# Pooled attention with an expert layer: order of the first loads and layouts, and the last block's additions

## The chip, the cores and the metric

The program runs on one core of one Trainium2 chip. The metric is the device time of one execution in microseconds (us); smaller is better. Work is done by TensorE (PE; its weight loads are shown as PEld), VectorE (DVE), ScalarE (ACT) and GpSimd (POOL). SyncE (SP) issues most of the DMA transfers, ACT issues a few at the start.

## The reference

Queries are averaged in pairs along the sequence, attention with a softmax over 1152 keys follows, and the result of the eight heads of each batch entry goes through an expert layer with a squared rectifier.

```python
def _attn_ref(q, k, v):                      # 4 x 8 x 1152 x 64 each
    q_pool = q.reshape(B, H, S // factor, factor, D).mean(axis=3)
    scores = scale * np.matmul(q_pool, k.transpose(0, 1, 3, 2))
    scores = scores - np.max(scores, axis=-1, keepdims=True)
    attn = np.exp(scores)
    attn = attn / (np.sum(attn, axis=-1, keepdims=True) + 1e-09)
    return np.matmul(attn, v).astype(np.float32)
...
def _moe_ref(x, w_in, w_out, s, b):          # x: 2304 x 512, d_ff 2048
    h = x @ w_in
    r = np.maximum(h, 0.0)
    g = s * (r * r) + b
    return (g @ w_out).astype(np.float32)
```

## The kernel before

**Precision.** Most products are made of three passes on rounded parts: a number is split into a high part (rounded by ACT or POOL, `hi_of`, L285 and L287) and a low part (the difference, on DVE or POOL).

**Attention.** The 32 heads are worked on as 16 pairs. For each pair, `load_k` (L525) and `load_q` (L533) bring raw keys (four transfers) and queries (eight), in packets of 128 bytes. `prep_pair` adds the two queries of a pair of rows (`qs`), transposes keys (`ka`, `kb`, one half each) and queries (`qt`) on DVE, rounds them (`ha`, `hb`, `qh` on ACT; `qm` and `qz` are copies of the queries laid out for the maxima), and takes the low parts on POOL (`kl`, `ql`). `lay` (L579 to L582) then copies high and low parts with transfers into `kk` (keys) and `qq` (queries) of one head: these are the operands of the scores.

**Maxima.** Before a head's scores can be exponentiated, each query needs a bound. `max_unit` (L633, L634) multiplies one tile of queries with 384 keys and reduces the result to a maximum on DVE; a pair has 27 such units (9 tiles of queries by 3 blocks of keys), the first 15 belong to the pair's first head. When a head's units are done, `shift` reduces them to `c` (L652) and two small transfers (L657, L658) write `c` into a row of that head's `qq`. **The scores of a head therefore wait for the transfers of its `c`.** `begun(n)` is the number of units done before step n; 22 of pair 0's units are done ahead of step 0, and 27 before step 3.

**The main loop** has a step for each head and block of 128 keys (9 steps a head). In it stand four score products (`score_step`, L672, into `s`), the products with the values for the block three steps earlier (`value_step`, L704 to L714, into `o`), and some units of the next pair's maxima. Everything on an engine, and everything that SP issues, runs in the order in which the code recorded it: an instruction that waits holds up all that are behind it on that engine. Preparations of later pairs are put into steps by tables: `LD = 4` means that in step 4 the raw keys and queries of pair 2 are issued (`load_k(2)`, `load_q(2)`). Work given to `later(k, fn)` is recorded k ticks later, and a step ends with a tick. A transfer also waits for an earlier one when it takes over that one's completion semaphore (eight are used in turn).

**Start.** Keys, queries and values of pair 0 are loaded in this order, six of the eight transfers of queries by ACT. POOL clears buffers meanwhile. Then come all preparations of pair 0, the loads of pair 1, the layouts of heads 0 and 1, and the units ahead. Head 0's `c` is sent by ACT, all later ones by SP.

**Expert layer and tail.** The last stage works on pairs of expert blocks: `pair1` (L404 to L435) makes the rounded operands, `pair2` (L452) seven products into the four accumulators `a`, `b`, `m`, `z` (tiles `seven`), and after the last pair of a token block `drain` (L465) adds them on DVE into `yq`, nine additions, and two transfers (L482) write the block out. In the last token block nothing else is left to run beside this.

Of the kernel before, what the change touches and what calls it, by code (L numbers as in the profile page):

```python
# [52 lines left out]
LAGS = 2  # L53
# [7 lines left out]
def attention_moe_kernel(ctx: ExitStack, tc: tile.TileContext, q, k, v, w_in, w_out, s_in, b_in, out):  # L61
# [243 lines left out]
    class Moe:  # L305
# [89 lines left out]
        def pair1(self, blk, n):  # L395
# [43 lines left out]
        def pair2(self, blk, n, first, last):  # L439
# [5 lines left out]
            todo = ((a, 0, sums[0], w[1]), (a, 512, own[0], w[2]), (b, 0, own[1], w[3]), (b, 512, sums[1], w[4]), (m, 0, sums[4], w[0]), (m, HD, sums[3], w[5]), (z, 0, sums[2], w[6]))  # L445
            for at, (y, to, (gh, gl), (wh, wl)) in enumerate(todo):
# [6 lines left out]
                if last:  # L453
                    self.drain(blk, at)
# [3 lines left out]
        def drain(self, blk, at):  # L458
# [5 lines left out]
            def add(out, b, op=ALU.add):  # L464
                nc.vector.tensor_tensor(out=out, in0=out, in1=b, op=op)  # L465

            if at == 1:
                add(quad[:, 0::3], both(a))
                add(quad[:, 1], a[:, 512:512 + HD])
                add(quad[:, 1], a[:, :HD], ALU.subtract)  # L470
            elif at == 3:
                add(quad[:, 0::3], both(b))
                add(quad[:, 2], b[:, :HD])
                add(quad[:, 2], b[:, 512:512 + HD], ALU.subtract)
# [47 lines left out]
    def load_k(p):  # L522
        kraw[p] = ap.tile([P, NB, 32], F32, tag="kraw", name=f"kraw{p}")
        for r, b, h, c in quarters(p):
            nc.sync.dma_start(kraw[p][r], k[b, h, :, c].rearrange("(j t) i -> t j i", t=32))  # L525
# [14 lines left out]
    def prep_pair(p):  # L540
# [17 lines left out]
        def k_hi(part, last):  # L558
            hi_of(nc.scalar if p < 3 else nc.gpsimd, kh[:, part], kT[:, part])
            if last:  # L560
                khs[p] = kh
# [5 lines left out]
        def q_blocks():  # L567

            for h in range(2):
                r = slice(h * D, (h + 1) * D)  # L570
                hi_of(nc.scalar if p == 0 else nc.gpsimd, qzs[p % 2][r, h].rearrange("p (t m) -> p t m", t=NT4), qT[r, :NT4 * P].rearrange("p (m t) -> p t m", t=NT4))

        def lay(h):
# [3 lines left out]
            ks = ((f32(kk[D:P, 0, :]), kT[r]), (f32(kk[0:D]), f32(kh[r]).unsqueeze(1).to_broadcast([D, 2, S])))  # L577
            for dst, src in ks[::-1] if hd == 0 else ks:
                nc.sync.dma_start(dst, src)  # L579
            nc.sync.dma_start(f32(qq[0:D, 0, :]), f32(qh[r]))  # L580
            nc.sync.dma_start(f32(qq[D:P, 0, :]), f32(qh[r]))
            nc.sync.dma_start(f32(qq[0:D, 1, :]), qT[r])  # L582
# [10 lines left out]
            "qz": q_blocks,  # L593
            "kl": lambda: nc.gpsimd.tensor_tensor(out=kT, in0=kT, in1=f32(kh), op=ALU.subtract),
# [22 lines left out]
    def max_unit(u, pool, tag):  # L617
# [4 lines left out]
        t, e = divmod(w, NE)  # L622
# [16 lines left out]
    def begun(n):  # L639

        u = (n + AHEAD) * NU // 18
        if n > 0:
# [3 lines left out]
    def shift(hd, pm, full, rest):  # L646
# [7 lines left out]
        eng = nc.scalar if hd == 0 else nc.sync  # L654
# [104 lines left out]

    load_k(0)  # L760
    load_q(0)
    load_v(0)

# [21 lines left out]
    zeros(1)  # L785
    constants(1)
# [7 lines left out]
    prep_v(0)  # L794
    ones(1)
    constants(2)
    for n in range(AHEAD):
        for u in range(begun(n - AHEAD), begun(n - AHEAD + 1)):
            max_unit(u, *((ps_m, "m") if u % 2 == 0 else (ps_s, "s")))
        tick()  # L800
        if n == 11:
# [180 lines left out]
```

## Time and profile before

| | us |
|---|---|
| runs (three) | 917.39, 917.93, 918.42; median 917.93 |
| the profiled execution | 918.26, of which the span is 916.3 |
| PE, DVE, POOL, ACT busy in the span | 893.6 (98%), 690.8 (75%), 631.2 (69%), 570.3 (62%) |
| granted TensorE clock, mean | 0.995 |
| first product on PE, last product on PE (start) | 12.19, 910.16 |

The profile lists what each engine did, when, and what released an engine that had waited. "Granted clock" is the share of full speed at which TensorE ran: 1.00 is 2.4 GHz, 0.50 is 1.2 GHz. A DMA's row shows how long the issuing queue was occupied, not the transfer; "to landing" is from issue to arrival.

### The profile page before, as it was taken

The numbers are of one execution on the slowest core, as the hardware profiler recorded it, in microseconds if no ns is written. First come the engines' busy times: TensorE is split into PE (matmuls) and PEld (weight loads), VectorE is DVE, ScalarE is ACT, GpSimd is POOL, SyncE is SP. The second block draws the span as 40 slices with busy tenths as digits, with TensorE's granted clock in tenths as the row PEclk, the third lists the DMA queues.
The fourth block names the chain that finished last, engine by engine and source line by source line (L and its number), as shares of the span: only waits on it lengthen the run. The fifth ranks groups of instructions, "written<-read, shape, count | busy, mean of one in ns | idle before, by whom it ended". The sixth has DMA issues, their size and how long they took to land.

```text
span 916.3 us, 17038 instructions
## 1 busy us (share of the span) xinstructions
PE 893.6 (98%) x6036; PEld 830.5 (91%) x6036; DVE 690.8 (75%) x1271; ACT 570.3 (62%) x1050; POOL 631.2 (69%) x535
## 2 busy tenths in 40 slices
PE   4999999999999999999999999999999999999996
PEld 2889999999999999999998899989999999999996
DVE  5787888888888888888875678789884456666665
ACT  2766666767676767667668677766664445444442
POOL 8577766887788778877857667569985445554542
PEclk9999999999999999999999999999999999999999
DMA  8899788878877897888572465757643222222111
GB/s 151 158 170 197 156 171 168 158 167 165 175 149 172 162 180 145 174 161 168 125 176 73 151 207 177 250 179 223 185 139 121 87 69 71 70 70 69 48 47 47
DMA packets 255796, 131.22 MB, mean 143 GB/s; under 512 B 203872, under 2 KB 227424, under 8 KB 255712
## 3 DMA queue, kind: packets, MB, share of 16 engines
q1 hardware_dynamic: 251936, 129.69, 60.2%
q8 instruction: 48, 0.79, 0.4%
q10 hardware_dynamic: 3776, 0.45, 0.3%
q14 instruction: 36, 0.29, 0.1%
HBM read 68.68 MB, written 18.87 MB: 96 GB/s over the span
## 4 chain that ended last, share of the span: by engine, by line
PE 86%; DVE 7%; ACT 2%; POOL 1%; issue 1%; DMA 0%; SPq 0%; POOLq 0%; ACTq 0%; DVEq 0%
PE s L672 14%; PE y L379 11%; PE h L352 11%; PE h L404 11%; PE seven L452 9%; PE o L704 8%; PE m L633 8%; PE o L712 5%; PE o L714 5%; PE o L710 5%; DVE pm L634 2%; DVE yq L465 1%; DVE lt L732 1%; DVE rr L742 1%; DVE pl L687 1%
## 5 line engine op out<-in xcount | busy, mean ns | idle before, releaser
L634 DVE TENSOR_REDUCE pm<-m 128x1 f32<-128x384 f32 x432 | 226.2, 544 | 55.5 <-PE m L633 49.6
L672 PE MATMUL s<-qq,kk 128*128 128x288 f32 x1152 | 214.9, 309 | 1.2 <-ACT pe L676 0.4
L672 PEld LDWEIGHTS s<-qq,kk 128*128 128x128 f32 x1152 | 175.5, 189 | 11.8 <-DVE pl L687 1.3
L681 ACT ACTIVATE ph<-s 128x576 fp32r<-128x576 f32 x192 | 125.2, 652 | 96.3 <-PE s L672 95.7
L687 POOL TENSOR_TENSOR pl<-pe,ph 128x576 fp32r<-128x576 f32 x64 | 90.7, 1417 | 97.6 <-ACT pe L684 75.2
L633 PE MATMUL m<-kh,qz 128*128 128x384 f32 x384 | 154.5, 416 | 1.1 <-DVE pm L634 0.3
L704 PE MATMUL o<-pe,vf 128*128 128x288 f32 x384 | 120.6, 405 | 0.0
L687 DVE TENSOR_TENSOR pl<-s,ph 128x576 fp32r<-128x576 f32 x128 | 96.1, 751 | 31.6 <-ACT s L684 23.3
L712 PE MATMUL o<-ph,vl 128*64 128x288 f32 (+1 forms) x384 | 113.5, 295 | 0.2 <-POOL vl L608 0.2
L714 PE MATMUL o<-pl,vv 128*128 128x288 f32 x384 | 113.4, 295 | 0.1
L710 PE MATMUL o<-ph,vv 128*128 128x288 f32 x384 | 113.2, 295 | 0.0
L352 PE MATMUL h<-x,wih 128*128 128x256 f32 x576 | 106.8, 283 | 0.8 <-DVE gl L366 0.7
L404 PE MATMUL h<-x,wih 128*128 128x256 f32 x576 | 104.2, 281 | 0.0
L352 PEld LDWEIGHTS h<-x,wih 128*128 128x128 f32 x576 | 93.7, 190 | 7.7 <-DVE gl L366 1.9
L432 POOL TENSOR_TENSOR cl<-c,ch 128x640 fp32r<-128x640 f32 x36 | 56.4, 1567 | 57.5 <-ACT ch L428 57.5
L633 PEld LDWEIGHTS m<-kh,qz 128*128 128x128 f32 x384 | 72.7, 192 | 18.3 <-DVE pm L634 10.2
L404 PEld LDWEIGHTS h<-x,wih 128*128 128x128 f32 x576 | 88.7, 188 | 0.2
L676 ACT ACTIVATE pe<-s 128x576 f32<-128x576 f32 x96 | 62.6, 652 | 36.1 <-PE s L672 32.3
L684 ACT ACTIVATE s<-s 128x576 f32<-128x576 f32 x128 | 83.3, 651 | 0.0
L352 PE MATMUL h<-x,wil 128*128 128x256 f32 x288 | 81.6, 283 | 0.0
L330 POOL TENSOR_TENSOR x<-xr,x 128x1024 fp32r<-128x1024 f32 x27 | 65.0, 2406 | 23.7 <-ACT x L285 23.7
L404 PE MATMUL h<-x,wil 128*128 128x256 f32 x288 | 81.1, 282 | 0.0
(282 smaller groups left out, 2184.6 us busy)
## 6 DMA issues: line engine op xcount, KB each, us to landing
kk<-kh SPq DMA_DIRECT2D x32, 576.0 KB, 5.7
kraw<-in_k_dram SPq DMA_DIRECT2D x64, 144.0 KB, 3.4
vf<-in_v_dram SPq DMA_DIRECT2D x32, 288.0 KB, 4.2
kk<-kT SPq DMA_DIRECT2D x32, 288.0 KB, 3.5
qq<-qh SPq DMA_DIRECT2D x64, 144.0 KB, 5.6
xr<-xd SPq DMA_DIRECT2D x18, 512.0 KB, 3.9
qraw<-in_q_dram SPq DMA_DIRECT2D x122, 72.0 KB, 2.6
wsti<-in_moe_w_in_dram SPq DMA_DIRECT2D x13, 512.0 KB, 4.2
```

What stands on the lines that cost most here:

```text
L352: nc.tensor.matmul(h[:, :TB], st[:, c, :], mv[:, c, :], start=(n == 0), stop=(n == 3 * NC - 1))
L379: nc.tensor.matmul(y[:, :DM], st[:, ts_], mv, start=(first and n == 0), stop=(last and n == 2))
L404: nc.tensor.matmul(h[:, e * TB:(e + 1) * TB], st[:, c, :], mv[:, c, :], start=(k == 0), stop=(k == 3 * NC - 1))
L633: nc.tensor.matmul(ps[:, :KB], st, khs[p][:, e * KB:(e + 1) * KB], start=True, stop=True)
L634: nc.vector.tensor_reduce(out=pms[p][:, col, e:e + 1], in_=ps[:, :KB], axis=AX.X, op=ALU.max)
L672: nc.tensor.matmul(ps[:, a, :HALF], kk[:, i, j * P:(j + 1) * P], qq[:, i, a], start=(i == 0), stop=(i == 1))
L681: nc.scalar.activation(ph, ps[:, :, :HALF], AF.Exp, scale=SCALE)
L687: fresh.append(lambda: eng.tensor_tensor(out=pl, in0=full, in1=f32(ph), op=ALU.subtract))
L704: nc.tensor.matmul(o[:, :HALF], vfs[hd % 2][:, j], ph[:, a], start=first, stop=last)
L710: nc.tensor.matmul(o[:, :HALF], vv[:, j], ph[:, a], start=first, stop=False)
L712: nc.tensor.matmul(o[0:vl.shape[2], :HALF], vl[:, j], ph[:, a], start=False, stop=False)
L714: nc.tensor.matmul(o[:, :HALF], vv[:, j], pl[:, a], start=False, stop=last)
```

## The change

Four things are edited.

- **Start.** `load_q(0)` comes ahead of `load_k(0)`, alternating between SP and ACT; the keys come in two halves. The preparation is ordered queries first, then the first half of the keys. After the second unit of maxima the second half is prepared and head 0's layout is issued in pieces, then the loads of pair 1's keys. One of the two `qz` copies moves to POOL, the buffers of heads 1 and 2 are cleared later, and `load_q(1)` and head 1's layout follow `c` of head 0.
- **Maxima of head 0** go by key blocks: all five query tiles with keys 0 to 383, then the next block. Head 0's `c` is now sent by SP.
- **Units ahead.** `begun` gives 20 units ahead of step 0 instead of 22; 21, 23, 24, 26 and 27 are done before steps 1 to 5, so pair 0's last unit is in step 4, where it was in step 2.
- **Tail.** In every block `pair2` takes the two products with `ah`, `al` first. In the last pair of the last block `cl` is made on DVE; three of the nine additions go to POOL, from copies that ACT makes of the accumulators, and each half of the rows is written out when it is done.

```diff
-            todo = ((a, 0, sums[0], w[1]), (a, 512, own[0], w[2]), (b, 0, own[1], w[3]), (b, 512, sums[1], w[4]), (m, 0, sums[4], w[0]), (m, HD, sums[3], w[5]), (z, 0, sums[2], w[6]))
+            todo = ((a, 512, own[0], w[2]), (b, 0, own[1], w[3]), (a, 0, sums[0], w[1]), (b, 512, sums[1], w[4]), (m, 0, sums[4], w[0]), (m, HD, sums[3], w[5]), (z, 0, sums[2], w[6]))
...
-                nc.gpsimd.tensor_tensor(out=cl, in0=c, in1=f32(ch), op=ALU.subtract)
+                (nc.vector if end else nc.gpsimd).tensor_tensor(out=cl, in0=c, in1=f32(ch), op=ALU.subtract)
...
+            def single(k, bank, tag):
+                plus, minus, eng = bank[:, (k == 1) * 512:(k == 1) * 512 + HD], bank[:, (k == 2) * 512:(k == 2) * 512 + HD], nc.vector
+                if end and k == 2:
+                    add(quad[:, k], minus, ALU.subtract)
+                if end:
+                    t = self.q.tile([P, 5 * P if tag == "c" else 2 * TB], F32, tag=tag, bufs=1, name=f"end{k}")
+                    if k == 1:
+                        nc.scalar.activation(t[:, :2 * HD].rearrange("p (e d) -> p e d", d=HD), both(bank), AF.Copy)
+                        minus = t[:, :HD]
+                    else:
+                        nc.scalar.activation(t[:, :HD], plus, AF.Copy)
+                    plus, eng = t[:, (k == 1) * HD:(k == 1) * HD + HD], nc.gpsimd
+                add(quad[:, k], plus, ALU.add, eng)
+                if not end or k == 1:
+                    add(quad[:, k], minus, ALU.subtract, eng)
-            if at == 1:
+            if at == 2:
                 add(quad[:, 0::3], both(a))
-                add(quad[:, 1], a[:, 512:512 + HD])
-                add(quad[:, 1], a[:, :HD], ALU.subtract)
+                single(1, a, "c")
...
-                for i in range(TB // P):
-                    row = blk * TB + i * P
-                    later(1, lambda i=i, row=row: nc.sync.dma_start(out[row:row + P, :], acc[:, i]))
+            if at > 4:
+                i = at - 5
+                later(1, lambda: nc.sync.dma_start(out[blk * TB + i * P:blk * TB + (i + 1) * P, :], acc[:, i]))
...
-                eng = nc.sync if p or (r.start == P - 32) else nc.scalar
+                eng = nc.sync if p or e == 0 else nc.scalar
...
-        t, e = divmod(w, NE)
+        t, e = divmod(w, NE) if u >= (NT4 + 1) * NE else divmod(w, NT4 + 1)[::-1]
...
         u = (n + AHEAD) * NU // 18
+        if n < 7:
+            u = min(u, 20 + max(0, n * 3 // 2))
...
-        eng = nc.scalar if hd == 0 else nc.sync
+        eng = nc.sync
...
-    load_k(0)
     load_q(0)
+    load_k(0, 2)
     load_v(0)
...
-    for name in ("ka", "ha", "kb", "hb", "qs", "qt", "qm", "qz", "qh", "kl", "ql"):
+    for name in ("qs", "qt", "qm", "qz0", "ka", "ha", "qh", "kla"):
         prep[name]()
-    load_k(1)
-    prep["l0"]()
-    load_q(1)
-    prep["l1"]()
...
             max_unit(u, *((ps_m, "m") if u % 2 == 0 else (ps_s, "s")))
+            if u == 1:
+                for name in ("kb", "hb", "ql", "klb", "l0"):
+                    prep[name]()
+                load_k(1)
...
         tick()
+        if n == 10:
+            assert holds["c", 0] == 0
+            load_q(1)
+            prep["l1"]()
```

Three places in the order of instructions. **DVE at the start of the program**, before; `kraw0`, `qraw0` are the raw loads of pair 0, `m0_0` is the first unit of maxima:

```order
L586 STREAM_TRANSPOSE kT0_139<-kraw0_109 128x576
L588 STREAM_TRANSPOSE kT0_139<-kraw0_109 128x576
L587 TENSOR_TENSOR qs0_141<-qraw0_114 128x576
L590 STREAM_TRANSPOSE qT0_140<-qs0_141 128x576
L634 TENSOR_REDUCE pm0_190<-m0_0_191 128x1
```

The same place, DVE after:

```order
L625 TENSOR_TENSOR qs0_140<-qraw0_109 128x576
L628 STREAM_TRANSPOSE qT0_139<-qs0_140 128x576
L624 STREAM_TRANSPOSE kT0_138<-kraw0_118 128x576
L676 TENSOR_REDUCE pm0_152<-m0_0_153 128x1
L676 TENSOR_REDUCE pm0_152<-m0_1_156 128x1
L626 STREAM_TRANSPOSE kT0_138<-kraw0_118 128x576
```

The transpose of the second half of the keys moved behind the first two reductions, the queries moved to the front.

**SP between the layout of head 1 and that of head 2**, before; `kk1`, `qq1` are head 1's operands, `c1` its maxima, `kraw2` and `qraw2` the loads of pair 2:

```order
L582 DMA qq1_98<-qT0_140 64x576
L538 DMA vf1_104<-in_v_dram 128x9x64
L804 DMA sb_71<-in_moe_s_dram 128x1
L805 DMA sb_71<-in_moe_b_dram 128x1
L657 DMA qq1_98<-c1_315 1x128x4
L658 DMA qq1_98<-c1_315 1x64x1
L525 DMA kraw2_355<-in_k_dram 32x36x32 x4
L533 DMA qraw2_360<-in_q_dram 32x18x32 x8
```

The same place, SP after:

```order
L620 DMA qq1_98<-qT0_139 64x576
L555 DMA vf1_104<-in_v_dram 128x9x64
L853 DMA sb_71<-in_moe_s_dram 128x1
L854 DMA sb_71<-in_moe_b_dram 128x1
L543 DMA kraw2_360<-in_k_dram 32x36x32 x4
L550 DMA qraw2_365<-in_q_dram 32x18x32 x8
L701 DMA qq1_98<-c1_352 1x128x4
L702 DMA qq1_98<-c1_352 1x64x1
```

The two transfers of `c1` moved from ahead of the twelve loads of pair 2 to behind them.

**DVE's last instructions of the program**, before; `yq8_27` is the last block's sum, `seven0` to `seven3` are the accumulators `a`, `b`, `m`, `z`:

```order
L431 TENSOR_TENSOR gl8_14s_11935<-rr8_3_11930,gh8_14s_11934 128x256
L465 TENSOR_TENSOR yq8_27_11703<-yq8_27_11703,seven0_9699 128x2x256
L465 TENSOR_TENSOR yq8_27_11703<-yq8_27_11703,seven0_9699 128x256 x2
L465 TENSOR_TENSOR yq8_27_11703<-yq8_27_11703,seven1_9700 128x2x256
L465 TENSOR_TENSOR yq8_27_11703<-yq8_27_11703,seven1_9700 128x256 x2
L465 TENSOR_TENSOR yq8_27_11703<-yq8_27_11703,seven2_9701 128x2x256
L465 TENSOR_TENSOR yq8_27_11703<-yq8_27_11703,seven2_9701 128x256
L465 TENSOR_TENSOR yq8_27_11703<-yq8_27_11703,seven3_9702 128x256
```

The same place, DVE after (`cl8_3` is the last block's `cl`):

```order
L431 TENSOR_TENSOR gl8_14s_11942<-rr8_3_11937,gh8_14s_11941 128x256
L432 TENSOR_TENSOR cl8_3_11940<-c8_3_11938,ch8_3_11939 128x640
L465 TENSOR_TENSOR yq8_27_11710<-yq8_27_11710,seven0_9706 128x2x256
L465 TENSOR_TENSOR yq8_27_11710<-yq8_27_11710,seven1_9707 128x2x256
L465 TENSOR_TENSOR yq8_27_11710<-yq8_27_11710,seven1_9707 128x256
L465 TENSOR_TENSOR yq8_27_11710<-yq8_27_11710,seven2_9708 128x2x256
L465 TENSOR_TENSOR yq8_27_11710<-yq8_27_11710,seven2_9708 128x256
L465 TENSOR_TENSOR yq8_27_11710<-yq8_27_11710,seven3_9709 128x256
```

`cl8_3` moved from POOL to DVE, and three of DVE's nine additions moved to POOL.

## Rows read from the trace of the kernel before

**Rows 1.** The page's chain that ended last, shares of the span.

```profile
PE 86%; DVE 7%; ACT 2%; POOL 1%; issue 1%; DMA 0%; SPq 0%; POOLq 0%; ACTq 0%; DVEq 0%
```

**Rows 2.** Timeline of the start: start, us, engine, line, operation, [idle before].

```profile
8.53 0.78 DVE L586 STREAM_TRANSPOSE kT<-kraw 128x576 f32<-128x576 f32 x1 [8.53 <-DMA kraw<-in_k_dram]
...
9.34 1.34 ACT L285 ACTIVATE kh<-kT 128x576 fp32r<-128x576 f32 x2 [3.59 <-DVE kT L586]
...
12.19 1.30 PE L633 MATMUL m<-kh,qm 128*128 128x384 f32 x3 [12.19 <-ACT qm L285]
...
12.88 7.06 DVE L634 TENSOR_REDUCE pm<-m 128x1 f32<-128x384 f32 x15 [1.46 <-PE m L633]
...
19.98 0.17 DVE L652 TENSOR_REDUCE c<-pm 128x5 fp32r<-128x15 f32 x1
...
20.82 0.60 ACTq L658 DMA_DIRECT2D qq<-c  x1
...
22.53 1.33 PE L672 MATMUL s<-qq,kk 128*128 128x288 f32 x4 [0.24 <-DVE pm L634]
```

**Rows 3.** Timeline of SP's queue between 19 and 43 us.

```profile
19.44 6.32 SPq L533 DMA_DIRECT2D qraw<-in_q_dram  x8
25.80 0.51 SPq L579 DMA_DIRECT2D kk<-kT  x1
...
33.85 0.53 SPq L657 DMA_DIRECT2D qq<-c  x1
34.42 0.60 SPq L658 DMA_DIRECT2D qq<-c  x1
35.12 2.87 SPq L525 DMA_DIRECT2D kraw<-in_k_dram  x4
38.09 5.29 SPq L533 DMA_DIRECT2D qraw<-in_q_dram  x8
```

**Rows 4.** What SP's queue waited for, 20 to 75 us (total, times, longest).

```profile
SPq L533 <- DMA qq<-c: 2.2, 1, 2.2
```

**Rows 5.** DMA issues between 30 and 50 us: count, size, us to landing.

```profile
qq<-c SPq DMA_DIRECT2D x1, 0.2 KB, 2.7
```

**Rows 6.** Windows: PE, PEld, DVE, ACT, POOL busy, granted clock, DMA share, GB/s.

```profile
19.00:19.25 0.25, 0.25 (x2) 0.18 (x1) 0.25 (x2) 0.00 (x0) 0.19 (x2) 0.78 0.94 212
22.50:35.00 12.50, 11.55 (x60) 10.29 (x61) 9.21 (x16) 8.77 (x17) 4.14 (x5) 0.86 0.87 171
25.75:26.00 0.25, 0.25 (x3) 0.25 (x2) 0.19 (x1) 0.25 (x1) 0.00 (x0) 0.56 0.69 108
40.00:60.00 20.00, 19.65 (x127) 17.86 (x126) 16.61 (x31) 13.71 (x26) 16.30 (x13) 1.00 0.92 182
913.00:914.00 1.00, 0.00 (x0) 0.00 (x0) 0.00 (x0) 0.00 (x0) 0.00 (x0) 0.72 0.55 207
```

**Rows 7.** Timeline of PE where head 1's scores begin.

```profile
37.62 0.70 PE L672 MATMUL s<-qq,kk 128*128 128x288 f32 x4
38.15 0.65 PE L704 MATMUL o<-pe,vf 128*128 128x288 f32 x2
```

**Rows 8.** Timeline of the last 20 us.

```profile
896.64 1.46 DVE L431 TENSOR_TENSOR gl_10s<-rr,gh_10s 128x256 fp32r<-128x256 f32 x1
...
906.31 1.54 POOL L432 TENSOR_TENSOR cl<-c,ch 128x640 fp32r<-128x640 f32 x1 [1.19 <-ACT ch L428]
...
907.91 0.39 PE L452 MATMUL seven<-woh,cl 128*128 128x256 f32 x1 [1.11 <-POOL cl L432]
...
908.69 4.25 DVE L465 TENSOR_TENSOR yq<-yq,seven 128x512 f32<-128x512 f32 x9 [2.95 <-PE seven L452]
...
912.63 0.81 SPq L482 DMA_DIRECT2D out_dram<-yq  x2
```

**Rows 9.** DVE's additions after 908.6 us by form: count, busy us, mean ns.

```profile
L465 DVE TENSOR_TENSOR yq<-yq,seven 128x256 f32<-128x256 f32 x6 | 2.4, 418 | 0.1
L465 DVE TENSOR_TENSOR yq<-yq,seven 128x512 f32<-128x512 f32 x3 | 2.0, 682 | 2.9 <-PE seven L452 2.9
```

More of the change, by code (lines that the diff above doesn't have):

```diff
@@ L393, in store, with pair1 @@
                 later(3, lambda: nc.sync.dma_start(parts[row], yo))
-        def pair1(self, blk, n):
+        def pair1(self, blk, n, end):
             xh, xl = self.x[blk]
@@ L437, in pair1, with pair2 @@
                 later(at, fn)
-        def pair2(self, blk, n, first, last):
+        def pair2(self, blk, n, first, last, end):
             ah, al, ch, cl = self.g[blk, SW[1] + 2 * n]
@@ L520, in quarters, with load_k @@
                 yield r, (2 * p + h) // H, (2 * p + h) % H, slice(g * 32, (g + 1) * 32)
-    def load_k(p):
+    def load_k(p, parts=1):
         kraw[p] = ap.tile([P, NB, 32], F32, tag="kraw", name=f"kraw{p}")
-        for r, b, h, c in quarters(p):
-            nc.sync.dma_start(kraw[p][r], k[b, h, :, c].rearrange("(j t) i -> t j i", t=32))
+        n = NB // parts
+        for i in range(parts):
+            for at, (r, b, h, c) in enumerate(quarters(p)):
+                eng = nc.scalar if parts > 1 and i and at % 2 else nc.sync
+                eng.dma_start(kraw[p][r, i * n:(i + 1) * n], k[b, h, i * n * 32:(i + 1) * n * 32, c].rearrange("(j t) i -> t j i", t=32))
     def load_q(p):
@@ L559, in k_hi @@
             hi_of(nc.scalar if p < 3 else nc.gpsimd, kh[:, part], kT[:, part])
-            if last:
-                khs[p] = kh
+            khs[p] = kh
         def q_hi():
@@ L565, in q_hi, with q_blocks, both, k_lo @@
             qhs[p] = qh
[L567 to L571, printed above, removed]
+        def q_blocks(h):
+            r = slice(h * D, (h + 1) * D)
+            hi_of(nc.scalar if p == 0 and h else nc.gpsimd, qzs[p % 2][r, h].rearrange("p (t m) -> p t m", t=NT4), qT[r, :NT4 * P].rearrange("p (m t) -> p t m", t=NT4))
+        def both():
+            q_blocks(0)
+            q_blocks(1)
+        def k_lo(part=slice(0, S)):
+            nc.gpsimd.tensor_tensor(out=kT[:, part], in0=kT[:, part], in1=f32(kh[:, part]), op=ALU.subtract)
         def lay(h):
@@ L576, in lay, with k_hi_to, k_lo_to, q_hi_to @@
             r = slice(h * D, (h + 1) * D)
[L577 to L582, printed above, removed]
+            def k_hi_to(part):
+                nc.sync.dma_start(f32(kk[0:D, :, part]), f32(kh[r, part]).unsqueeze(1).to_broadcast([D, 2, part.stop - part.start]))
+            def k_lo_to(part):
+                nc.sync.dma_start(f32(kk[D:P, 0, part]), kT[r, part])
+            def q_hi_to():
+                nc.sync.dma_start(f32(qq[0:D, 0, :]), f32(qh[r]))
+                nc.sync.dma_start(f32(qq[D:P, 0, :]), f32(qh[r]))
+            if hd == 0:
+                k_hi_to(lo)
+                q_hi_to()
+                k_hi_to(hi)
+                k_lo_to(lo)
+                nc.sync.dma_start(f32(qq[0:D, 1, :]), qT[r])
+                k_lo_to(hi)
+            else:
+                k_lo_to(slice(0, S))
+                k_hi_to(slice(0, S))
+                q_hi_to()
+                nc.sync.dma_start(f32(qq[0:D, 1, :]), qT[r])
             holds["k", hd % 3] = hd
@@ L592, in prep_pair @@
             "qh": q_hi,
[L593 to L594 removed]
+            "qz": both,
+            "qz0": lambda: q_blocks(0),
+            "qz1": lambda: q_blocks(1),
+            "kla": lambda: k_lo(lo),
+            "klb": lambda: k_lo(hi),
+            "kl": k_lo,
             "ql": lambda: nc.gpsimd.tensor_tensor(out=qT, in0=qT, in1=f32(qh), op=ALU.subtract),
@@ L941, in attention_moe_kernel @@
                 moe.acc[blk] = moe.fetch_y(blk)
-            for _ in moe.pair1(blk, n):
+            for _ in moe.pair1(blk, n, m == len(pairs) - 1):
                 tick()
```

24 lines of the change are left out of this document (12 added, 12 removed).

## The prediction, made before the changed kernel ran

> **What bounds the kernel now.** I read the chain of waits first: TensorE holds 86% of it, the other engines little [rows 1]. So between start and end time is won or lost only where PE stands still or runs slowly. That leaves three places: the start until PE is fed, the joints between heads, where PE could wait for operands, and the end behind the last product. I read each on the timeline.
>
> At the start DVE waits until 8.53 us for the keys; the first unit of maxima is on PE at 12.19, its reduction at 12.88; 15 reductions take 7.06; `c` of head 0 is made at 19.98, its second transfer is issued by ACT at 20.82, and the first scores stand at 22.53 [rows 2]. At the joint to head 1, SP sends `c` of that head at 33.85 and 34.42, the second landing 2.7 us later, at 37.1 [rows 3, 5]. Head 1's scores begin at 37.62 without a wait [rows 7]. Half a microsecond of slack is all there is. SP's next work, the twelve loads of pair 2, stands from 35.12 to 43.4 [rows 3]. At the end PE waits for `cl`, which POOL makes in 1.54 us, and nine additions on DVE run from 908.69 to 912.9 with nothing beside them [rows 8].
>
> I sum against the profiled execution, 918.26 us (span 916.3), which is 0.33 above the median of 917.93; the last line is on the median's scale.
>
> **Start, a gain that is not kept.** All queries (590 KB) and half the keys (295 KB) now come ahead of DVE's first key transpose, and what came ahead of it before was 590 KB of keys mixed with most of the queries. I take the half to be there at 7.5. Then come a transpose of 0.78, one rounding of 0.67 (half of the 1.34 for two) and, because ACT has `qm` to make ahead of it, the first product at 9.4 (bounds 8.5 and 10.5) against 12.19 [rows 2]. The 15 reductions take the same 7.06, plus the second key transpose, 0.78, which now stands between them. So `c` is made at 9.4 + 0.7 + 7.06 + 0.78 = 17.9, 2.1 earlier. It is sent by SP behind the layout of head 0 and pair 1's keys, so it can land later than the 1.8 us that ACT's transfer needed (20.82 to about 22.6). I take the first scores at 20.8, 1.7 earlier (bounds 0.8 and 3). The 20 units ahead instead of 22 neither add nor remove work; the two units are done between scores. POOL's clearing of later buffers and `vl`, moved to behind the first units, cost nothing: POOL is busy for only 4.14 of the 12.5 us from 22.5 [rows 6]; without that cover each would delay the first values by its own length.
>
> **The joint to head 1, the deciding term.** Pair 0's last unit moves from step 2 to step 4. In step 4 the code first records the twelve loads of pair 2 and only at the tick the sending of `c1`; the order of SP shows `c1` behind them. Nothing overtakes on SP. Behind it wait PE's second and fourth score product of head 1, and behind those, PE working in order, everything. The time of `c1`, step by step: SP is through with `c0` at about 19.3 (17.9, made and issued, 1.2 for two issues). Eight loads of queries follow, 0.515 us each, since their 6.32 before holds 2.2 of waiting for `c0` [rows 3, 4], whose landing now concerns only the last two of them: 23.4, against 25.8. From there to the place where `c1` stood SP needed 33.85 - 25.80 = 8.05: 31.4. Then the twelve loads, from 35.12 to 43.4, or 8.3 us: 39.7. Then `c1`: 0.53 and 0.60, the second issued at 40.3 and landing 2.7 later [rows 3, 5]: 43.0. I take 42.8, since the loads follow the layout without the pause that `c1` made.
>
> Bounds: the twelve loads at 0.72 (keys, 2.87 for four [rows 3]) and 0.515 (queries) without waits are 7.0, so the second `c1` is issued at 39.0, and a landing takes 1.8 at best: 40.8. The layout ahead of them may wait less too; I set the bound at 40.0. A count of bytes says the same: from the landing of `c0` to that of `c1` SP now sends 0.59 MB (queries of pair 1), 1.33 (layout), 0.29 (values) and 1.18 (pair 2), 3.4 MB; at the 171 GB/s of 22.5 to 35 us [rows 6] that is 19.9 us, from about 21 to 41. The upper bound is 44, a landing 1 us slower.
>
> Before, the four products were over and the next one stood at 38.15 [rows 7]; now the fourth can begin at 42.8 and the next at 42.9. That is **+4.7** (bounds +2.0 and +6.0). It contains the start's gain already: PE would have come there at about 35.9 and stands idle for close to 7 us.
>
> **The clock behind the stall.** PE's clock was granted at 1.00 until the thin stretch of maxima, where it fell to 0.50 (1.2 GHz) at 19.2; it came back at 25.9 [rows 6], 3.4 us after the first scores [rows 2]. Behind the last product (its start is at 910.16) it had fallen again by 913.3 [rows 6]. With 7 idle us it falls in the stall, and the work behind it runs at half speed until it is back. If that takes the 3.4 us of the start, half of them are lost, 1.7; if it takes the whole 6.7 us of the low stretch, 3.4. I take **+2.0**, near the first row, as the product order there is dense. PE's small waits between 40 and 60 us, 20 less 19.65 busy [rows 6], mostly vanish because the other engines have caught up: **-0.3**.
>
> **The tail.** `cl` on DVE: 640 columns by the rate of 256 in 0.418 and 512 in 0.682 [rows 9] are 0.82; it can begin where POOL did, at 906.3, and is there at 907.1, not 907.85 [rows 8]. PE fills the time with the six products on `ah` and `al`, which needed no `cl`, and 19 products that began at 907.91 begin as 21 at 906.3: the last ends at about 908.9, 1.5 us earlier. DVE has six additions, three of 0.682 and three of 0.418, 3.3 us, where it had nine in 4.25; the first needs nine products, at 907.5: DVE is done at 910.7. Beside it ACT makes two copies, about 0.6 and 0.45 (0.67 for 576 columns [rows 2]), and POOL three additions of 256 columns, 0.62 each by its 1.54 for 640 [rows 8], in a chain 907.5 + 0.6 + 1.24, then 0.62: 910.3 with waits. The second output goes out at 910.7 instead of about 913.0 (912.63 is the first's). **-2.2**. If POOL's additions take twice as long, 1.24 each, the last is done at 911.8 and the output leaves 1.2 earlier than before: -1.2. The better end is -2.4.
>
> DVE and POOL do slow each other in this trace: one `gl` of 256 columns took 1.46 beside POOL's `cl` [rows 8], where additions of that width from an accumulator take 0.418 [rows 9]. The Trainium skill, SBUF — State Buffer, section "Who interferes with whom", says that a VectorE operation with two inputs in SBUF contends with a GpSimd operation that reads SBUF, and the loser waits for the whole instruction, while one with at most one input in SBUF does not contend. By that rule the additions here, with one input in PSUM, run freely, and the sum stays at -2.2; if every pair blocked as that `gl` did, about 1 us each for two of them would leave -0.2. No row here shows POOL's additions beside these.
>
> **Sum.** 918.26 + 4.7 + 2.0 - 0.3 - 2.2 = 922.5 for the profiled execution, 922.1 on the median's scale. I call it 922.
>
> **The rivals.**
>
> *The stall without the clock.* PE stands still as above but comes back at full speed. 918.26 + 4.7 - 0.3 - 2.2 = 920.5, or 920.1. Against it: the clock fell within 3 us of idle time at the end [rows 6].
>
> *A shorter stall.* The twelve loads issue at their shortest, `c1` lands at 40.0: +2.0, clock +1.7, tail -2.2, -0.3: 919.5, or 919.1. For it: SP reaches the loads earlier than before and has no other duty. Against it: eight semaphores in turn tie each load to an earlier landing, and bytes at 171 GB/s need until 41.
>
> *The start's gain is kept (faster).* `c1` lands before PE asks for it. Place: the same joint. It decides at 35.9: if 3.4 MB pass in the 15 us from 21, at 227 GB/s, there is no stall, and from then on PE is 1.7 ahead. 918.26 - 1.7 - 2.2 = 914.4, or 914.0. Against it: the mean was 171 GB/s in a stretch where the DMA engines were busy for 0.87 of the time [rows 6].
>
> *A worse stall.* `c1` at 44 and a clock that stays low for the full 6.7 us: +6.0 + 3.4 - 1.2 = 926.5, or 926.
>
> **How the numbers follow.** Forecast 0.60, no clock loss 0.15, shorter stall 0.10, gain kept 0.07, worse stall 0.08. The range leaves out the last two and reaches from just below the shorter stall to the forecast with its terms at the high ends: 918.5 to 925.5. A measurement of this kernel tells 0.2% from no change, 1.8 us, so 916.1 to 919.8 is "same". Faster is the gain kept, 0.07; same is the shorter stall, 0.10, with a little of the stall without clock loss, 0.12; slower is the rest, 0.81.
>
> **What would show it.** In the profile of the changed kernel: SP's two `c` transfers at about 39.7 and 40.3, behind four and eight loads; a wait of some 6 us of PE's line of scores on a DMA `qq<-c` between 36 and 43; a granted clock of 0.50 for some 4 us behind it; the first scores near 20.8; output transfers about 2 us closer to the last product. The prediction is wrong if PE shows no idle time between 36 and 43, which would mean that SP ran through the loads sooner than any row here lets me expect.

## The result and the profile after

| | before | changed |
|---|---|---|
| median (range), us | 917.79 (917.38 to 918.42) | 927.17 (926.71 to 927.90) |
| runs | 5 | 5 |
| profiled execution (span) | 918.26 (916.3) | 927.15 (925.4) |

The ratio is 1.0102 (95% interval 1.0091 to 1.0113): the changed kernel is 9.4 us slower. Slower was forecast, and by the mechanism that was forecast, but 927.17 lies above the range of 918.5 to 925.5.

**Where the time went.** In the chain of [rows 1] DMA and SP had no share; now they have 1% each. The page's list of costly groups (busy, mean ns | idle before, releaser) names the new wait: ahead of its score products PE was idle for 10.2 us, 9.3 of them until a transfer of `c`.

```profile
L716 PE MATMUL s<-qq,kk 128*128 128x288 f32 x1152 | 216.4, 310 | 10.2 <-DMA qq<-c 9.3
```

The start, to be laid beside [rows 2] (timeline: start, us, engine, line, operation, count, [idle before]):

```profile
6.18 0.76 DVE L625 TENSOR_TENSOR qs<-qraw 128x576 f32<-128x576 f32 x1 [6.18 <-DMA kraw<-in_k_dram]
...
7.83 1.28 ACT L285 ACT_TABLE_LOAD   x1 [7.83 <-DVE qT L628]
...
10.50 0.66 PE L675 MATMUL m<-kh,qm 128*128 128x384 f32 x1 [10.50 <-ACT kh L285]
...
13.67 0.69 PE L675 MATMUL m<-kh,qm 128*128 128x384 f32 x1 [1.17 <-ACT kh L285]
...
16.67 3.37 SPq L543 DMA_DIRECT2D kraw<-in_k_dram  x4
...
19.17 0.17 DVE L696 TENSOR_REDUCE c<-pm 128x5 fp32r<-128x15 f32 x1
...
20.14 0.95 SPq L701 DMA_DIRECT2D qq<-c  x1
...
21.14 0.60 SPq L702 DMA_DIRECT2D qq<-c  x1
...
22.66 0.61 PE L716 MATMUL s<-qq,kk 128*128 128x288 f32 x1 [1.27 <-DMA qq<-c]
```

DVE begins 2.3 us earlier (6.18 against 8.53), PE 1.7 earlier (10.50 against 12.19), and `c` of head 0 is made 0.8 earlier (19.17 against 19.98). But the three score products that need it begin at 22.66, where all four began at 22.53 before. Each step passes on less than it was given. The table load of ACT, 1.28 us, now stands behind its wait for `qT`; PE waits 1.17 for the second half of the keys; SP is busy with pair 1's keys until 20.04 and sends `c` a microsecond after it is made.

SP from the queries of pair 1 to `c` of head 1, to be laid beside [rows 3]:

```profile
21.78 4.36 SPq L550 DMA_DIRECT2D qraw<-in_q_dram  x8
26.19 0.51 SPq L602 DMA_DIRECT2D kk<-kT  x1
...
34.02 3.79 SPq L543 DMA_DIRECT2D kraw<-in_k_dram  x4
37.92 5.56 SPq L550 DMA_DIRECT2D qraw<-in_q_dram  x8
43.59 0.51 SPq L701 DMA_DIRECT2D qq<-c  x1
44.14 0.60 SPq L702 DMA_DIRECT2D qq<-c  x1
```

`c1` now goes out at 43.59 and 44.14 behind the twelve loads (33.85 and 34.42 ahead of them before); DVE had made it at 32.57. PE at head 1, answering [rows 7], and behind it the granted clock (windows: PE, PEld, DVE, ACT, POOL busy, clock, DMA share, GB/s):

```profile
37.42 0.29 PE L716 MATMUL s<-qq,kk 128*128 128x288 f32 x1
45.78 1.09 PE L716 MATMUL s<-qq,kk 128*128 128x288 f32 x3 [8.07 <-DMA qq<-c]
46.67 1.16 PE L748 MATMUL o<-pe,vf 128*128 128x288 f32 x2
...
49.23 1.12 PE L716 MATMUL s<-qq,kk 128*128 128x288 f32 x4
```

```profile
38.00:40.00 2.00, 0.00 (x0) 0.00 (x0) 0.00 (x0) 0.00 (x0) 2.00 (x2) 0.98 0.92 145
40.00:46.00 6.00, 0.22 (x1) 0.22 (x2) 0.00 (x0) 0.00 (x0) 2.50 (x3) 0.50 0.65 100
46.00:50.00 4.00, 4.00 (x13) 3.43 (x14) 1.09 (x3) 1.19 (x2) 0.00 (x0) 0.50 1.01 203
50.00:51.00 1.00, 1.00 (x8) 0.96 (x8) 1.00 (x3) 0.61 (x1) 0.00 (x0) 0.91 0.83 166
```

One score product runs, the other three wait 8.07 us. The first value product stands at 46.67, where it stood at 38.15 [rows 7]: +8.5. In the wait the clock falls to 0.50 (1.2 GHz), and the 4 us behind it run at that level: 13 products in 46 to 50, where the kernel before had 24. By the second and third block of head 1 the lag against before is 9.8 and 10.2 us, and it is still 10.1 at 914 us: nothing is caught up.

The tail, answering [rows 8]:

```profile
916.40 0.82 DVE L432 TENSOR_TENSOR cl<-c,ch 128x640 fp32r<-128x640 f32 x1 [0.53 <-ACT ch L428]
...
917.71 3.20 DVE L465 TENSOR_TENSOR yq<-yq,seven 128x512 f32<-128x512 f32 x6 [0.48 <-PE seven L452]
...
918.49 0.60 ACT L475 ACTIVATE end<-seven 128x512 f32<-128x512 f32 x1 [2.12 <-DVE yq L465]
...
919.16 2.21 POOL L465 TENSOR_TENSOR yq<-yq,end 128x256 f32<-128x256 f32 x3 [3.91 <-ACT end L475]
...
920.72 1.01 SPq L497 DMA_DIRECT2D out_dram<-yq  x2
```

From DVE's first step for the last pair (L422, at 914.51, and at 904.38 before) to the end of the span it takes 10.9 us instead of 11.9. So the span grew by 10.1 - 1.0 = 9.1, as it stands in the table.

### The profile page after: what moved, and what is told of

Its sections match the earlier page's. It is cut to its first block, busy times and chain, and to the rows that moved or that the text cites. A ratio compares the mean times of both kernels' runs of the same rounds, so it can differ in the third digit from the quotient of the medians.

```text
span 925.4 us, 17058 instructions
## 1 busy us (share of the span) xinstructions
PE 895.5 (97%) x6036; PEld 832.7 (90%) x6036; DVE 691.0 (75%) x1269; ACT 570.7 (62%) x1051; POOL 633.8 (68%) x539
## 4 chain that ended last, share of the span: by engine, by line
PE 92%; DVE 3%; ACT 2%; DMA 1%; POOL 1%; SPq 1%; issue 1%; POOLq 0%; DVEq 0%; ACTq 0%
PE s L716 16%; PE h L404 11%; PE y L379 11%; PE h L352 10%; PE seven L452 10%; PE o L748 9%; PE m L675 9%; PE o L756 5%; PE o L758 5%; PE o L754 5%; DVE pm L676 1%; SPq L550 1%; DMA qq<-c 1%; DVE lt L776 0%; DMA kraw<-in_k_dram 0%
## 5 line engine op out<-in xcount | busy, mean ns | idle before, releaser
L716 PE MATMUL s<-qq,kk 128*128 128x288 f32 x1152 | 216.4, 310 | 10.2 <-DMA qq<-c 9.3
```

The costliest lines, as they stand in the source:

```text
L716: nc.tensor.matmul(ps[:, a, :HALF], kk[:, i, j * P:(j + 1) * P], qq[:, i, a], start=(i == 0), stop=(i == 1))
```

## Experiments

Each ratio is to runs of the kernel before on the same chip (medians 918.36, 918.41 and 918.13 us); differences between two of these kernels are between their medians.

### Which part makes the stall

**Twelve loads a step later** (the changed kernel; `c1` goes ahead of them again):

```diff
-LD = 4
+LD = 5
```

> The changed kernel with one number changed: the raw loads of pair 2 are recorded in step 5 instead of step 4, so c1 stands ahead of them in SP's queue again. Theory A (the stall is c1's place in the queue): c1 is issued at about 34 us and lands at 37, head 1's scores begin at 37.4 without a wait, the clock stays at 1.00, and 8.4 + 1.8 us go: about 916.9, that is 0.9 below the kernel before, which is the tail's gain alone. Theory B (the DMA engines are full, c1 cannot land much sooner wherever it is issued): it lands at 40 or later, and more than 2.5 us of the stall stay: 919.5 or more.

Measured: 917.94 (917.25 to 918.26), ratio 0.9993 (0.9985 to 1.0002). `c1` is sent ahead of the loads, which follow at 35.18:

```profile
33.98 0.51 SPq L701 DMA_DIRECT2D qq<-c  x1
34.53 0.60 SPq L702 DMA_DIRECT2D qq<-c  x1
```

```profile
37.54 0.70 PE L716 MATMUL s<-qq,kk 128*128 128x288 f32 x4
```

Head 1's four score products run together, and PE has no wait for `c` between 34 and 50 us. One number gives back 9.2 of the 9.4 us: the stall, with the slower clock behind it, is the whole loss. But start and tail together are worth only 0.4 against the kernel before, about half of what was expected, and the interval holds no change as well.

**The units alone** (the kernel before with the new `begun` and nothing else):

```diff
         u = (n + AHEAD) * NU // 18
+        if n < 7:
+            u = min(u, 20 + max(0, n * 3 // 2))
```

> The kernel before with one edit: the new rule for the units ahead (20 before step 0, the last unit of pair 0 in step 4). Theory A: this alone puts c1 behind the twelve loads of pair 2 on SP; its second transfer is issued at about 43.5, PE waits some 8 us at head 1's first scores and runs at half speed for 4 us behind that: 917.8 + 10 = about 928. A rival (the new start with its other order of loads is needed for the stall): under 922.

Measured: 928.07 (927.03 to 928.13), ratio 1.0103 (1.0089 to 1.0117). In the old start, too, the three products wait:

```profile
42.21 0.53 SPq L659 DMA_DIRECT2D qq<-c  x1
...
44.26 1.09 PE L674 MATMUL s<-qq,kk 128*128 128x288 f32 x3 [7.43 <-DMA qq<-c]
```

Two added lines that name no transfer cost 9.7 us. The new loads and layouts are not needed for it.

**Only four loads ahead** (the changed kernel, pair 2's queries a step later):

```diff
             if n == LD:
                 load_k(2)
+            if n == LD + 1:
                 load_q(2)
```

> The changed kernel with only the eight query loads of pair 2 moved from step 4 to step 5; its four key loads stay in step 4. c1 then stands behind four loads instead of twelve. Theory A (the stall is the time that SP spends on the loads ahead of c1): the key loads take 3.8 us as in the changed kernel, c1 is issued at 37.9 and 38.4 and lands at 40.4, TensorE waits 2.7 us instead of 8.1. Against e1_loads_step5 (917.9) that is +2.8 if the granted clock holds, 920.7, and +1.8 more if it falls as in the changed kernel, 922.5. Rival (the wait is for bytes that pair 2's keys put ahead, or for something that is not SP's order): a wait of 5 us or more, or none.

Measured: 922.53 (920.06 to 923.30), ratio 1.0045 (1.0031 to 1.0059).

```profile
34.17 3.81 SPq L543 DMA_DIRECT2D kraw<-in_k_dram  x4
38.09 0.67 SPq L701 DMA_DIRECT2D qq<-c  x1
...
41.44 1.09 PE L716 MATMUL s<-qq,kk 128*128 128x288 f32 x3 [3.33 <-DMA qq<-c]
```

The trace is that of an execution of 922.16 us. In it the granted clock is 0.50 from 42 to 44 us, as Theory A's second figure, 922.5, has it; one of the five, at 920.06 and with a higher mean clock (0.999), lies nearer the first, 920.7. With 0, 4 and 12 loads ahead of `c1` PE waits 0, 3.3 and 8.1 us and the time is 917.9, 922.5 and 927.2. The stall goes with SP's order, load by load.

**`c1` from another queue** (the changed kernel; SP's loads stay where they are):

```diff
-        eng = nc.sync
+        eng = nc.scalar if hd == 1 else nc.sync
```

> The changed kernel with head 1's c sent by ACT instead of SP; the units, the loads and their steps are as in the changed kernel. In the changed kernel DVE made c1 at 32.57 and SP issued it at 43.59. Theory A (only SP's queue holds c1): ACT issues it by 36, it lands by 38 at the latest, the wait of 8.1 us goes, the clock stays at 1.00, and the time is that of e1_loads_step5, 917.9, give or take 0.7. Rival (c1 is late by the later units themselves, or its bytes wait behind those of the twelve loads): a wait of 2 us or more stays and the time is over 920.

Measured: 920.25 (918.80 to 920.86), ratio 1.0023 (1.0014 to 1.0032). Head 1's scores no longer wait for `c`, so the rival's cause falls, though its time (over 920) came. The time is 2.3 over what Theory A expected. What took it stands on ACT, and then on PE:

```profile
32.93 0.53 ACTq L701 DMA_DIRECT2D qq<-c  x1
33.50 0.62 ACTq L702 DMA_DIRECT2D qq<-c  x1
34.16 0.65 ACT L725 ACTIVATE ph<-s 128x576 fp32r<-128x576 f32 x1 [2.65 <-POOL qz L287]
...
35.28 0.50 ACT L285 ACTIVATE qm<-qT 64x64 fp32r<-64x64 f32 x2
...
35.83 0.45 PE L675 MATMUL m<-kh,qm 128*128 128x384 f32 x1 [2.41 <-ACT qm L285]
```

ACT stands for 2.65 us up to the end of its two issues, and they go out as soon as DVE has made `c1` (32.68). (The row names POOL as the releaser; in the changed kernel the same exponential ran at 31.44, 0.21 us after the one before it, when PE had its scores.) The exponentials and pair 1's `qm` come behind the issues; `qm` starts at 35.28, where the changed kernel had it at 32.56, and PE waits 2.41 for it. Against Theory A the clock falls as well, to 0.50 from 38 to 40 us, behind this wait. Head 1's scores stand at 41.65, 4.1 later than in e1_loads_step5, and 2.3 of that are left between the medians. A transfer that waits for its data holds up what stands behind it on the engine that issues it: loads on SP, exponentials on ACT.

### What the clock costs

**TensorE kept busy in the stall** (the changed kernel with 60 extra score products there, their results overwritten):

```diff
         for i in range(2):
+                if hd == 1 and j == a == i == 0:
+                    for _ in range(60):
+                        nc.tensor.matmul(ps[:, 0, :HALF], kk[:, 0, :P], qq[:, 0, 0], start=True, stop=True)
```

> The changed kernel, with 60 extra score products (results thrown away) put ahead of head 1's first score product, so that TensorE works through most of the wait for c1 instead of standing still. c1 itself is not moved. Theory A (stall 8.4 us, and 1.8 us more because the granted clock fell to 0.50 in the stall): head 1's second to fourth products still at about 45.8, but the granted clock stays at 1.00 behind them, and head 1's next blocks stand 1.5 to 2 us earlier than in the changed kernel (s of block 1 at about 47.7 instead of 49.2); time 925.4. Rival (the 1.8 us are work of other engines that had piled up, not the clock): 927.2 as the changed kernel.

Measured: 925.34 (924.89 to 926.07), ratio 1.0076 (1.0063 to 1.0088): 1.83 under the changed kernel. Windows and PE's timeline:

```profile
38.00:44.00 6.00, 6.00 (x48) 6.00 (x47) 0.12 (x1) 0.00 (x0) 4.71 (x4) 1.00 0.90 142
46.00:50.00 4.00, 4.00 (x28) 3.71 (x27) 2.98 (x6) 2.20 (x4) 0.00 (x0) 1.00 0.97 190
```

```profile
37.62 8.06 PE L718 MATMUL s<-qq,kk 128*128 128x288 f32 x60
45.52 0.69 PE L719 MATMUL s<-qq,kk 128*128 128x288 f32 x4
...
47.38 0.69 PE L719 MATMUL s<-qq,kk 128*128 128x288 f32 x4
```

The 60 products fill the stall to its end, and head 1's four products follow them without a wait for `c`, within 0.3 us of where they stood (45.52 against 45.78; SP sent the second `c1` 0.5 earlier, at 43.66). The clock stays at 1.00. The next block stands at 47.38 instead of 49.23, 1.85 earlier, and the one behind it at 49.85 instead of 52.11, 2.26 earlier. Less the 0.26 by which head 1 begins earlier, the clock is 1.6 at the one block and 2.0 at the other. That the clock is a cause, not only a sign, is shown here.

### Where the start's gain goes

**`c0` sent by ACT, as before the change** (e1_loads_step5 and this line):

```diff
-        eng = nc.sync
+        eng = nc.scalar if hd == 0 else nc.sync
```

> As the first, and c0 of head 0 is sent by ACT again instead of SP. Theory C (the start's gain, PE's first product 1.7 us earlier, is lost because c0 waits in SP's queue behind pair 1's key loads, issued at 20.14 though made at 19.34): ACT issues at 19.4, it lands by 21.6, the first scores are whole at 21.6 instead of 22.66, and the time is 1.0 us below the first run, about 915.9. Theory D (c0 waits in the DMA engines behind the keys' bytes, not in the queue): landing near 22.5 as before, no difference to the first run.

Measured: 917.31 (916.90 to 918.06), ratio 0.9988 (0.9980 to 0.9997). The second transfer is issued at 20.00 instead of 21.07, but head 0's remaining products start at 22.30 instead of 22.67:

```profile
20.00 0.60 ACTq L702 DMA_DIRECT2D qq<-c  x1
...
22.30 1.09 PE L716 MATMUL s<-qq,kk 128*128 128x288 f32 x3 [0.88 <-DMA qq<-c]
```

A free queue sends `c0` a microsecond earlier; two thirds of it are lost on the way, since this transfer takes 2.5 us to land and SP's, in e1_loads_step5, 1.8. Neither theory holds alone: C expected 21.6, D no difference. The time is 0.6 under e1_loads_step5.

**Pair 1's keys behind `c0`** (e1_loads_step5, and `load_k(1)` taken from where unit 1 is done to ahead of `load_q(1)`):

```diff
         if n == 10:
             assert holds["c", 0] == 0
+            load_k(1)
             load_q(1)
```

> As e1_loads_step5 (pair 2's loads in step 5), and the loads of pair 1's keys moved behind the two transfers of head 0's c. Theory D (c0 is late because pair 1's key loads stand ahead of it, on SP and as bytes in the DMA engines): SP issues c0 at about 19.3 and 19.8, it lands by 21.6, the first scores are complete at about 21.6 instead of 22.67, and the time is 1.0 under e1: 916.9. Rival (the landing of so small a transfer is some 2.5 us whatever stands ahead, and what comes later is bound by pair 1's preparation): first scores at 22.3, time 917.6 or more.

Measured: 919.95 (919.11 to 921.22), ratio 1.0017 (1.0009 to 1.0026). The step that was expected took place: head 0's four products stand at 21.13 without a wait for `c`. So the keys' bytes and issues were what held `c0`. But the time is 2.0 over e1_loads_step5, on the rival's side. The gain of 1.5 us is more than spent at the next joint: PE waits 1.8 us for `qm` of pair 1, whose queries now come later, and 0.8 for `c1`.

**The old number of units, with the new start and tail:**

```diff
-        if n < 7:
-            u = min(u, 20 + max(0, n * 3 // 2))
```

> The changed kernel with the old number of maxima ahead (22 units ahead of step 0, 27 before step 3); pair 2's loads stay in step 4. Theory A (the later units alone put c1 behind the twelve loads): c1 stands ahead of the loads again, no wait at head 1, granted clock 1.00 from about 30 us. Then the rest is the start and the tail. If the start's rearrangement is worth nothing (head 0's scores wait for c0 until 22.6, and the two more units lie in that wait), the time is that of the tail alone, 916.5. Rival (the new start itself costs about 1.4 us, which is the difference between e1_loads_step5 and e3_tail_alone): 918.0. If there is a stall still, Theory A falls: 920 or more.

Measured: 917.81 (917.38 to 919.20), ratio 0.9995 (0.9986 to 1.0003). No stall, as Theory A expected, and the rival on the start is right: 917.81 is 1.3 over the tail alone (916.54, below). By these medians the new start is not merely worthless without the stall, it costs 1.3; where, is left open (at the end of the next section).

**All repairs of the start together** (e7_units_as_before, pair 1's keys behind `c0`, and ACT's table loaded early):

```diff
+    warm = ap.tile([P, 1], F32, tag="warm", name="warm")
+    nc.gpsimd.memset(warm, 0.0)
+    nc.scalar.activation(warm, warm, AF.Copy)
     nc.gpsimd.memset(f32(qm), 0.0)
```

> As e7_units_as_before, pair 1's key loads moved behind c0, and ACT made to load its function table at the beginning, beside the first loads, by one activation on a 128x1 tile. Expected: first product at about 9.4 instead of 10.5; the second half of the keys is there no sooner, so c0 is made only some 0.3 us sooner, 18.9; it lands by 21.4, first scores complete at 21.5 or when unit 21 is done; 915.4. If the key loads and the table load were not what held c0, 916.5 as expected of e7; if pair 1's preparation is late instead (its keys come 3 us later), a new wait of the units of pair 1 and 917 or more.

Measured: 919.49 (918.11 to 921.82), ratio 1.0012 (1.0003 to 1.0021); the profiled execution, 921.39, is one of the longer ones. The start is the fastest of all, head 0's four products at 21.07. And then:

```profile
27.65 0.17 DVE L694 TENSOR_REDUCE c<-pm 128x5 fp32r<-128x15 f32 x1
...
35.46 0.51 SPq L699 DMA_DIRECT2D qq<-c  x1
36.02 0.60 SPq L700 DMA_DIRECT2D qq<-c  x1
...
39.74 1.06 PE L714 MATMUL s<-qq,kk 128*128 128x288 f32 x3 [3.18 <-DMA qq<-c]
```

PE comes to head 1 at 36.27, 1.3 earlier than in the kernel before. `c1`, made at 27.65, leaves SP at 35.46, behind the twelve loads and the layout of pair 1, and lands only at 39.7: a wait of 3.18, with the clock at 0.50 behind it. That joint, and not the start, sets when head 1 runs.

**One piece of the start without the rest** (e3_tail_alone, below, with the queries prepared ahead of the second half of the keys):

```diff
-    for name in ("ka", "ha", "kb", "hb", "qs", "qt", "qm", "qz", "qh", "kl", "ql"):
+    for name in ("ka", "ha", "qs", "qt", "qm", "kb", "hb", "qz", "qh", "kl", "ql"):
```

> e3_tail_alone with one thing of the new start: the queries of pair 0 are prepared ahead of the second half of the keys; the loads, the units and the transfers are as before the change. Expected: first product at about 10.6 instead of 11.9, but the second unit waits for the second half of the keys until 12.2, so head 0's c is made some 0.4 us earlier, the first scores at 21.9 instead of 22.24, and the time is 916.2, hardly to be told from 916.5. Rival (an earlier head 0 meets head 1's c as late as before, so that nothing is left of it): 916.5 or more, with a wait at head 1's first scores.

Measured: 917.70 (917.29 to 918.70), ratio 0.9997 (0.9988 to 1.0006), 1.2 over e3_tail_alone: a miss, and not by the rival, for there is no wait at head 1's first scores. With the old loads DVE stands 0.80 us before the queries, while the second half of the keys, which e3_tail_alone transposes there at 8.89, waits behind them:

```profile
9.72 0.76 DVE L602 TENSOR_TENSOR qs<-qraw 128x576 f32<-128x576 f32 x1 [0.80 <-DMA vf<-in_v_dram]
```

The row names the load of the values, which SP issues behind the queries. The first product is no earlier (12.06, after 11.91 in e3_tail_alone), and `c0` is made at 20.23, after 19.70.

### What the tail is worth

**The tail alone** (the kernel before with the edits of `pair1`, `pair2` and `drain`):

```diff
-                nc.gpsimd.tensor_tensor(out=cl, in0=c, in1=f32(ch), op=ALU.subtract)
+                (nc.vector if end else nc.gpsimd).tensor_tensor(out=cl, in0=c, in1=f32(ch), op=ALU.subtract)
...
-            todo = ((a, 0, sums[0], w[1]), (a, 512, own[0], w[2]), (b, 0, own[1], w[3]), (b, 512, sums[1], w[4]), (m, 0, sums[4], w[0]), (m, HD, sums[3], w[5]), (z, 0, sums[2], w[6]))
+            todo = ((a, 512, own[0], w[2]), (b, 0, own[1], w[3]), (a, 0, sums[0], w[1]), (b, 512, sums[1], w[4]), (m, 0, sums[4], w[0]), (m, HD, sums[3], w[5]), (z, 0, sums[2], w[6]))
...
+                    plus, eng = t[:, (k == 1) * HD:(k == 1) * HD + HD], nc.gpsimd
```

> The kernel before with the tail of the changed kernel alone (order of the seven products, cl of the last pair on DVE, three additions on GpSimd, output by halves). If the tail is worth what the two traces show (the end 10.13 us later before it, 9.1 at the end of the span): -1.0, about 916.8. If the predicted 2.2 are there and something else ate them: 915.6.

Measured: 916.54 (915.89 to 917.21), ratio 0.9981 (0.9972 to 0.9990), 1.8 us under the kernel before. It is the fastest kernel of this study, ahead of both.

**All nine additions left on DVE** (e3_tail_alone without copies and without additions on GpSimd):

```diff
-                if end and k == 2:
-                    add(quad[:, k], minus, ALU.subtract)
-                if end:
...
-                    plus, eng = t[:, (k == 1) * HD:(k == 1) * HD + HD], nc.gpsimd
                 add(quad[:, k], plus, ALU.add, eng)
-                if not end or k == 1:
-                    add(quad[:, k], minus, ALU.subtract, eng)
+                add(quad[:, k], minus, ALU.subtract, eng)
```

> e3_tail_alone (the tail alone, 916.5) with all nine additions back on DVE and no copies on ACT; cl on DVE and the new order of products stay. It divides the tail's gain. If each part is worth what the trace of e3_tail_alone shows: the last product stands where it does there (1.2 earlier than before), DVE's nine additions end at about 912.2 instead of POOL's end at 911.5, so 917.2. If the additions on GpSimd give nothing (they wait for ACT's copy, which waits for DVE), 916.5. If they carry most of the gain, 918.

Measured: 916.99 (916.28 to 917.45), ratio 0.9987 (0.9978 to 0.9996). DVE's nine additions run from 907.78 to 912.02:

```profile
907.78 4.24 DVE L465 TENSOR_TENSOR yq<-yq,seven 128x512 f32<-128x512 f32 x9 [0.48 <-PE seven L452]
```

So `cl` on DVE and the order of products bring most of the tail's gain, 1.1 us against the kernel before; the additions on GpSimd bring 0.4 to 0.7 more (the first between the two medians, the second between their gains), which is little above what two medians of this kernel can tell apart.

## Why the prediction came out as it did

**Bound, place, mechanism: right.** Time was lost at the joint to head 1, by `c1` behind the twelve loads, with PE idle and the clock down. e1, e2 and e9 show it: the cause can be taken away, made alone, and made in part.

**The joint, +4.7 forecast, +8.5 measured: the term that failed.** I had SP done with `c0` at 19.3; it was 21.7. Of these 2.4 us, `c0` was made 1.3 later than I had it (19.17 for 17.9), SP was busy 0.8 longer, and the two issues took 1.6 for 1.2. Three of the start's steps did not pass on their gain: ACT's table load, which stood beside the loads before (4.47 to 5.75) and which I did not follow to its new place; PE's wait for the second half of the keys; and pair 1's keys, through which SP was busy until 20.04. I had seen that SP sends `c0` behind them, drew from it only that `c0` could land later, and kept 19.3 as the point from which all that follows is counted. In e8_all, with the table loaded early and the keys behind `c0`, the first product stands at 9.86 instead of 10.50 and SP is done with `c0` at 19.9: these two steps were 1.85 of the 2.4. (The first score product stood at 20.78, where I had "the first scores", but by chance: it is the one that does not wait for `c0`.) The chain then ran on as worked out: the stretch from the first layout transfer to the loads of pair 2 took 7.8 (forecast 8.05). The twelve loads took 9.5 where before they took 8.3 [rows 3], so the second `c1` went out at 44.14 (forecast 40.3); 1.6 later, where I had allowed 2.5, PE went on, at 45.78 (forecast 42.8). That is 3.0 of the missing 3.8. The other 0.8 is what waits: I had named the second and the fourth product, but left only the fourth to run behind `c1`. PE works in order, so three were left, and at half speed they took until 46.67.

My bounds for this term varied loads and landing and held the chain ahead of them fixed, though I had given the first product bounds of 8.5 to 10.5, and it came at the upper one. With `c0` as late as the kernel before has it (ACT was through with it at 21.4), which the text had reason to allow, the upper end of the stall would have been about 46 and that of the range about 927.6.

**The clock, +2.0: right.** 1.6 to 2.0 by e5_busy_joint, some 0.4 of it in the three products at half speed that the joint's 8.5 holds already.

**Catching up, -0.3: not seen.** The lag is 10.2 us at 52 us and 10.1 at 914.

**The tail, -2.2: too good by 0.4 to 1.2.** -1.8 in e3_tail_alone, about -1.0 in the changed kernel's trace. The last product is 1.5 earlier, as worked out, and DVE's six additions took 3.20 (3.3). What was missed is on the other two engines. ACT's first copy waits for DVE's first wide addition, from the same accumulator, and starts at 918.49, 0.8 after that addition began, and POOL's additions took 0.72 each, not 0.62. So POOL ends the chain, at 921.37, 0.5 after DVE. The transfers out, 2.5 us to landing after 2.2, take some more.

**DVE beside POOL.** DVE's additions ran at 686 and 417 ns, as in [rows 9], in the changed kernel's last 8 us; four of the six stand beside POOL's, which begin at 919.16:

```profile
L465 POOL TENSOR_TENSOR yq<-yq,end 128x256 f32<-128x256 f32 x3 | 2.1, 724 | 4.0 <-ACT end L475 3.9
L465 DVE TENSOR_TENSOR yq<-yq,seven 128x512 f32<-128x512 f32 x3 | 2.1, 686 | 0.6 <-PE seven L452 0.5
L465 DVE TENSOR_TENSOR yq<-yq,seven 128x256 f32<-128x256 f32 x3 | 1.2, 417 | 0.0
```

The Trainium skill, SBUF — State Buffer, section "Who interferes with whom", says that a VectorE operation with at most one input in SBUF does not contend with GpSimd, outside its two-port modes. The trace agrees with 686 and 417 ns against 682 and 418 without POOL; the case of every pair blocking, -0.2, did not come.

**The start, "a gain that is not kept": right in the heading, wrong in the sum.** I carried it into the joint as an SP that is through with pair 1's queries 2.4 us earlier than before (23.4 against 25.8); it was 0.4 later, at 26.2 (the first layout transfer, at 26.19). e7_units_as_before puts the new start, without any stall, at a loss of 1.3, and in e6 and e8 a start that really is 1.5 earlier only waits longer at head 1.

**Left open.** Of the 1.3 us of the new start the two profiled executions show 0.3 at PE's last product (909.24 against 908.93) and 0.4 behind it; where the other 0.6 between the medians lies, no trace here shows. In e1_loads_step5, which has the new start too, the last product is not later at all (908.85). So the loss of 1.3 is measured, but its cause is not known. The times of e8_all fall into two groups, six from 918.1 to 918.9 and six from 920.1 to 921.8; whether the clock fell only in the second is not settled: the one trace is of an execution of that group, and the mean clocks listed for the two overlap (0.995 to 0.999, and 0.994 to 0.997).

## What to carry to other kernels

When work is put off by a step or two, look at what is recorded in that step ahead of its last instruction: here a transfer of 2 KB behind twelve loads on one queue cost 8.1 us of waiting, and PE's busy share moved only from 98% to 97%. Follow the chain ahead of a stall with the same care as the stall, every step with its own bounds; a term counted from a point that is not sure is no surer than that point. And before a start is made faster, find the next place where head and queue meet: here an earlier start was worth nothing as long as `c1` left SP at 34 to 35 us.

## What the runs showed of the hardware

**The granted clock can read 1.00 where products take half-speed times.** In the changed kernel the clock is listed as 1.00 from 12 to 27 us, and yet 384-column products have a median of 602 ns between 10 and 20 us (first row) and 335 ns between 30 and 38 (second; min/median/max in ns):

```profile
L675 PE MATMUL m<-kh,qz x17: 522/602/686, 11.0 to 19.9; 128*128 128x384 f32 x17
...
L675 PE MATMUL m<-kh,qz x3: 333/335/342, 29.9 to 37.0; 128*128 128x384 f32 x3
```

The weight loads ahead of them take 289 ns in the first stretch and 188 in the second. In the kernel before, where the column reads 1.00 from 13 to 19 us, such products have a median of 443 ns and weight loads 186; where it reads 0.50, behind that, they have 667 and 288. So 602 and 289 belong to the lower level (1.2 GHz). At the beginning of these programs the durations, of the weight loads above all, are the better witness of the level.

**A small transfer sent earlier need not land as much earlier.** The 2 KB of `c` took from 1.9 to 3.9 us to land in these traces. Issuing `c0` 1.07 us earlier from an idle queue (e4_step5_c0_act), with SP's loads of keys still going out, let the products start 0.37 us earlier; with those loads behind it (e6_k1_behind_c0) they had no wait for it.
